# Host-packed projection and gate tiles, and the second pair's loads behind the first pair's hash, in a fused bucketed-attention and mixture-of-experts kernel

## The chip, the cores and the metric

The kernel runs on one core of one Trainium2 chip. The metric is the device time of one execution in microseconds (us), the median of several runs; lower is better. Engines are named as in the profile: PE is TensorE's matmul side and PEld its weight loads, DVE is VectorE, ACT is ScalarE, POOL is GpSimd, SP is SyncE, which only issues transfers. SPq, ACTq and POOLq are the instruction sequencers of those engines, each of which works in program order.

## The reference

Attention with a bucket mask feeds a top-1 mixture of experts. Cut to what matters here:

```python
# q, k, v: (2, 8, 768, 64); proj: (64, 6)
q_bits = (einsum('bhsd,dk->bhsk', q, proj) > 0)          # six sign bits per query and key
q_bucket = sum(q_bits * 2 ** arange(6)); ...             # the same for k
scores = where(q_bucket == k_bucket, q @ k.T / 8, -1e9)
attn = softmax(scores) @ v
x = attn.transpose(0, 2, 1, 3).reshape(2, 768, 512)
logits = x @ w_gate                                      # 8 experts
local_gate = sigmoid(x @ w_local)                        # < 0.5: fresh expert, else that of the token before
out[b, s] = p[e] * (relu(x[b, s] @ w1[e]) @ w2[e])       # e: the chosen expert, p: softmax of logits
```

## The kernel before

The 16 heads of the two batches are worked as 8 pairs; a pair's two heads lie on partitions 0 to 63 and 64 to 127. For a pair p, `lx.p.0` and `lx.p.1` load the transposed queries and keys (`xq`, `xk`: 128 x 768 float32, 384 KB each) from HBM. `hash.p` multiplies both by the projections `hw` on PE (tile `hb`), takes the signs on DVE (`bt`, L184) and scales them on ACT into `br` (L187). `bd.p.j.a` copies the bits by four small transfers (39 KB each, L190) into rows 51 to 76 of the operands `b`, where the scores get the mask as a second matmul over 64 rows. `hi` and `lo` split queries and keys into a rounded part `hx` (L197 on DVE or POOL, L195 on ACT) and its remainder `lx` (L205). `s1` forms the scores of one query block for the row maximum (PE, L213; DVE reduces into `mx`, L222); `ma`, `mb`, `mc` turn the maximum into one more row of the operand `b`; `s2` forms the transposed scores, ACT takes their exponent into `pt`; `pv` multiplies by the values. `ug` multiplies a finished pair's output by `iw`, a tile that holds an identity of 128 columns and 18 columns of gate weights for each of four pairs (128 x 4 x 146), which yields the transposed output and the router's logits in one matmul. Routing, a scatter into slots by expert and the eight experts' two matmuls follow; that part fills the span from about 265 us.

Nothing is reordered at run time. One string, `ORDER`, lists every part in the order in which its instructions go into the engines' programs, and `MOVED` says where a part doesn't run on its first engine; `lx.1.0` and `lx.1.1` are issued from ACT's sequencer, `lx.0.0`, `lx.0.1`, `lhw` and `lcs` from SP's. `busy.2` stands for four matmuls on the zeroed tile `Fl` into a buffer nobody reads; ORDER has ten of them ahead of `hash.0` (40 matmuls) and eight between `hash.0` and `hash.1` (32). They go in order like any other PE instruction, so PE reaches a hash only after the fillers ahead of it. The first `busy` waits for the memset of `Fl` on DVE (L536), which stands behind the memset of `hw` (L535).

`hw` is a 128 x 32 tile: zeros, and the 64 x 6 projections twice for each head. Before, DVE clears it and `lhw` copies the projections in by two transfers, whose rows are runs of six floats. `iw` is cleared by POOL in `clear` (L560), its identities come by `iwc` (L572) and its gate columns by `iwl.1` and `iwl.0` (L568), long before the first `ug`.

`hash.0` takes its bits on DVE; behind it on DVE stand, in this order, `hi.0.0`, `ident`, `hi.1.1` (which reads `xk` of the second pair), `lo.0.1`, and the sign step of `hash.1`; then the reductions of `s1` begin. On PE, `hash.1` stands behind the 32 fillers and ahead of eight more and the first `s1`. On ACT, `hash.0` is followed by `bd.0.0.1` and `bd.0.0.0`, then by `hash.1`, whose `br` reuses the buffer that the four `bd.0` copies read.

Of the kernel before, what the change touches and what calls it, by code (L numbers as in the profile page):

```python
# [19 lines left out]


ORDER = """
lx.0.0 busy.2 lx.0.1 busy.2 busy.2 busy.2 lhw busy.2 busy.2 hi.0.1 busy.2 lcs busy.2 lx.1.0 lx.1.1 busy.2 busy.2
hash.0 hi.0.0 busy.2 ident busy.2 bd.0.1.1 busy.2 hi.1.1 lo.0.1 bd.0.0.1 lo.0.0 busy.2 bd.0.0.0 bd.0.1.0 busy.2
load_v.0.2 busy.2 busy.2 busy.2 hash.1 busy.2 busy.2 s1.0.0.0 busy.2 s1.0.0.1 s1.0.1.0 hi.1.0 lo.1.0 busy.2 lx.2.1
busy.2 s1.0.1.1 bd.1.0.0 busy.2 bd.1.0.1 s1.0.2.0 busy.2 s1.0.2.1 busy.2 busy.2 clear busy.2 busy.2 load_v.0.0
s1.0.3.0 ma.0.0 busy.2 s1.0.3.1 busy.2 busy.2 busy.2 bd.1.1.1 busy.2 mb.0.0 s1.0.4.0 busy.2 lx.2.0 load_v.0.3 s1.0.4.1
# [1 line left out]
s1.1.0.1 busy.2 s1.1.1.0 s2.0.2.0 s1.1.1.1 busy.2 load_v.0.5 load_v.0.1 s1.1.2.0 hi.2.1 s2.0.4.0 load_v.0.4 lx.3.0  # L29
mf.0.0 mc.0.1 s2.0.3.0 s1.1.2.1 busy.2 s2.0.1.1 bd.2.1.0 s1.1.3.0 s2.0.0.1 busy.2 s1.1.3.1 s2.0.4.1 s1.1.4.0 bd.2.1.1  # L30
busy.2 padd.0.1.0 s2.0.2.1 bd.2.0.1 s1.1.4.1 vsum.0 hi.2.0 s2.0.5.1 s1.1.5.0 s1.1.5.1 pv.0.0.0 bd.2.0.0 mf.0.1
pv.0.1.0 padd.0.1.1 pv.0.0.1 pv.0.1.1 s1.2.0.0 s2.0.5.0 s2.0.3.1 s1.2.0.1 s1.2.1.0 pv.0.2.0 padd.0.2.0 ma.1 lx.3.1 iwc
pv.0.2.1 hash.3 io flat.0.1 flat.0.0 mb.1 s1.2.1.1 padd.0.3.0 padd.0.2.1 s1.2.2.0 s1.2.2.1 hi.3.1 bd.3.0.0 bd.3.0.1
pv.0.3.0 pv.0.3.1 pv.0.4.1 hi.3.0 padd.0.3.1 lo.2.0 padd.0.4.1 mc.1 bd.3.1.1 padd.0.4.0 pv.0.4.0 pv.0.5.1 bd.3.1.0
s1.2.3.0 s2.1.1.0 padd.0.5.1 s2.1.0.0 s1.2.3.1 padd.1.1.0 s2.1.2.0 s2.1.2.1 s1.2.4.0 s2.1.1.1 padd.0.5.0 s2.1.0.1
# [1 line left out]
padd.1.2.1 pv.1.0.1 pv.1.0.0 pv.1.1.0 pv.1.2.0 s1.3.0.1 s2.1.5.1 padd.1.3.0 s2.1.4.1 s1.3.1.0 s2.1.4.0 lx.4.1 s2.1.3.1  # L37
load_v.1.3 ma.2 s1.3.1.1 sa.0 padd.1.3.1 hash.4 flat.1.1 flat.1.0 mb.2 sb.0 pv.1.1.1 pv.1.2.1 bd.4.1.0 lo.3.0 pv.1.3.0
pv.1.3.1 padd.1.4.1 s1.3.2.0 s1.3.2.1 lx.5.0 s1.3.3.0 pv.1.4.1 bd.4.0.0 bd.4.0.1 pv.1.4.0 mc.2 pv.1.5.1 pv.1.5.0
s1.3.3.1 hi.4.1 iwl.1 ot.1 s2.2.0.0 padd.1.4.0 s2.2.1.1 s1.3.4.0 lo.3.1 bd.4.1.1 padd.1.5.0 s2.2.2.1 iwl.0 s2.2.1.0  # L40
padd.1.5.1 s1.3.4.1 s1.3.5.0 lx.5.1 pv.2.0.0 s1.3.5.1 s2.2.3.0 hi.4.0 s2.2.3.1 s2.2.2.0 s2.2.0.1 s2.2.4.0 sa.1 ma.3
padd.2.1.0 hash.5 mb.3 padd.2.1.1 sb.1 padd.2.2.0 mc.3 pv.2.0.1 pv.2.1.1 pv.2.1.0 pv.2.2.0 mf.2 pv.2.2.1 s1.4.0.0
padd.2.2.1 s2.2.5.1 s2.3.0.0 s2.2.5.0 s2.2.4.1 bd.5.0.0 s2.3.0.1 padd.2.3.0 lo.4.0 lo.4.1 s1.4.0.1 load_v.1.1 lx.6.0
# [38 lines left out]
def moved(kind, *where):  # L82
    return MOVED.get(kind, {}).get(where, 0)
# [35 lines left out]
def tile_kernel(ctx, tc, qT, kT, v, proj, wg, w1, w2, cst, out):  # L119
    nc = tc.nc  # L120
# [21 lines left out]
    hw = const.tile([128, 32], F32, name="hw")  # L142
    iw = const.tile([128, 4, 146], F32, name="iw")
# [21 lines left out]
    def queue(kind, *where):  # L165
        return (nc.sync, nc.scalar, nc.gpsimd)[moved(kind, *where)]
# [365 lines left out]
    warm = const.tile([128, 1], F32, name="warm")  # L532
    nc.vector.memset(warm, 0.0)
    nc.scalar.activation(out=warm, in_=warm, func=ACTF.Exp)
    nc.vector.memset(hw, 0.0)  # L535
    nc.vector.memset(Fl.bitcast(F32), 0.0)  # L536
    for t in B[0]:
        nc.vector.memset(t.bitcast(F32), 0.0)
# [10 lines left out]
                                 rhs=Fl[64 * i:64 * i + 64, 0:384], tile_position=(64 * i, 0))  # L549

    def lhw():
        for h in range(2):
            queue("lhw").dma_start(out=hw[64 * h:64 * h + 64, 13 * h:13 * h + 12].rearrange("p (a c) -> p a c", a=2),
                                   in_=proj.unsqueeze(1).to_broadcast([64, 2, 6]))

    def lcs():
        queue("lcs").dma_start(out=cs, in_=cst[:, 0:200])

    def clear():
        nc.gpsimd.memset(iw, 0.0)  # L560
        nc.gpsimd.memset(ones, 1.0)
        nc.gpsimd.memset(zr.bitcast(F32), 0.0)

    def ident():
        nc.vector.tensor_copy(out=idr, in_=idf)

    def iwl(h):
        nc.sync.dma_start(out=iw[64 * h:64 * h + 64, :, 128 + 9 * h:137 + 9 * h],  # L568
                          in_=wg.rearrange("(a b d) e -> b d a e", b=2, d=64)[h])

    def iwc():
        nc.sync.dma_start(out=iw[:, :, 0:128], in_=cst[:, 8:136].unsqueeze(1).to_broadcast([128, 4, 128]))  # L572
    XA, HLE, OHE = [], [], []

    def onehot(tag, o):
# [19 lines left out]
    def ugh(p, half):  # L595
        ug(p, (half,))
    parts = {f.__name__: f for f in (
        bd, busy, clear, fill_slots, fill_some, flat, hash, hi, hle, ident, io, iwc, iwl, lcs, lhw, lo, load_v, lx,
        ma, mb, mc, mf, ohe, ot, oth, padd, pv, s1, s2, sa, sah, sb, sbh, split_h, split_l, step, ug, ugh, vsum, xa)}
    with tc.manual_schedule():  # L600
        for part in ORDER.split():
# [114 lines left out]
    with tc.If(n_ovf > 0):  # L716
# [7 lines left out]
        for b in range(2):  # L724
# [13 lines left out]
            for q in range(6):  # L738
                nc.gpsimd.indirect_dma_start(
                    out=xo[:, :], out_offset=bass.IndirectOffsetOnAxis(ap=so[:, q:q + 1], axis=0),  # L740
                    in_=XT[b][:, q], in_offset=None, bounds_check=5 * CAP - 1, oob_is_err=False)
# [33 lines left out]
```

## Time and profile before

| | us |
|---|---|
| median of 3 runs | 465.82 |
| the runs | 465.82, 466.21, 463.77 |
| device time of the profiled execution | 469.77 |
| its span, first to last instruction | 467.9 |
| PE busy in it | 437.9 (94%) |
| DVE busy in it | 303.4 (65%) |
| ACT busy, POOL busy in it | 203.4 (43%), 177.7 (38%) |

The profile is of one execution with the recorder on, and its device time is 3.95 us above the median of the others. All starts are counted from the span's first instruction. PE's busy share contains the fillers, so it doesn't say how much of PE's time does work.

### The profile page before, as it was taken

To read this page: it belongs to the slowest core of one execution; us is meant where nothing else is said; L and a number is where in the kernel's file an instruction comes from. 1 tells how busy PE (TensorE), PEld (TensorE's weight loads), DVE (VectorE), ACT (ScalarE), POOL (GpSimd) and SP (SyncE) were. 2 spreads that over 40 slices of the span, in tenths; PEclk is the share of its full clock that TensorE was granted. 3 is DMA by queue.
4 is the path that set the end of the run, shared out by engine and by line. 5 is a ranking of instruction groups with operands and counts; after the bars stand their busy time and mean duration, and the time that the engine had idled before them with its cause. 6 is when DMAs were issued, how large, how long until landed. Compare 5 with 4: busy or idle time off the path is not lost.

```text
span 467.9 us, 8276 instructions
## 1 busy us (share of the span) xinstructions
PE 437.9 (94%) x3316; PEld 343.4 (73%) x3316; DVE 303.4 (65%) x440; ACT 203.4 (43%) x277; POOL 177.7 (38%) x127
## 2 busy tenths in 40 slices
PE   8999999999999997999987389999999999999993
PEld 7886466776667484666554389898989988999982
DVE  4988895647676867887668948473737464647210
ACT  1144354643636171453245037473636363736310
POOL 3468456397579474255357530101010102010101
PEclk9999999999999998999999569999999999999998
DMA  3532111121050020402047529966676757666000
GB/s 144 163 107 72 50 59 47 37 62 48 6 170 2 35 73 2 181 1 87 36 156 242 179 69 317 322 194 222 207 237 206 230 191 255 222 217 223 36 2 31
DMA packets 41577, 60.17 MB, mean 129 GB/s; under 512 B 5949, under 2 KB 24093, under 8 KB 41536
## 3 DMA queue, kind: packets, MB, share of 16 engines
q1 hardware_dynamic: 38010, 50.54, 33.6%
q0 software_dynamic: 2272, 6.31, 3.6%
q10 hardware_dynamic: 1254, 2.76, 1.9%
q8 instruction: 27, 0.44, 0.4%
q14 instruction: 14, 0.11, 0.1%
HBM read 47.66 MB, written 11.56 MB: 127 GB/s over the span
## 4 chain that ended last, share of the span: by engine, by line
PE 44%; issue 36%; DVE 10%; POOL 4%; DMA 1%; ACT 1%; POOLq 0%; ACTq 0%; SPq 0%; DVEq 0%
PE s L213 21%; PE pv L275 13%; POOL out L698 4%; PE busy L548 3%; DVE rw L436 2%; PE ug L369 2%; DVE mx L222 2%; DVE sp L268 1%; PE st L327 1%; PE xt L612 1%; PE hb L181 1%; DMA PI<-xs 1%; DVE nf L229 1%; PE pv L282 1%; DVE lx L205 1%
## 5 line engine op out<-in xcount | busy, mean ns | idle before, releaser
L222 DVE TENSOR_REDUCE mx<-s 128x2 f32<-128x768 f32 x96 | 88.7, 953 | 37.1 <-PE s L213 36.4
L646 DVE TENSOR_TENSOR wl<-st,wh 128x1024 fp32r<-128x1024 f32 x60 | 71.8, 1221 | 61.5 <-ACT wh L645 61.4
L268 POOL TENSOR_TENSOR sp<-sp,pt 128x768 f32<-128x768 f32 x42 | 79.5, 1905 | 61.0 <-DVE sp L268 30.3
L261 ACT ACTIVATE pt<-s 128x768 f32<-128x768 f32 x96 | 73.2, 811 | 65.1 <-PE s L213 60.0
L645 ACT ACTIVATE wh<-st 128x1024 fp32r<-128x1024 f32 x64 | 66.5, 1059 | 46.9 <-DMA st<-w 27.0
L213 PE MATMUL s<-hx 64*128 64x384 f32 x384 | 71.3, 366 | 1.2 <-DVE mx L222 1.1
L676 PE MATMUL hps<-xH,wh 128*128 128x256 f32 x256 | 70.8, 278 | 0.7 <-ACT xH L709 0.7
L676 PE MATMUL hps<-xH,wl 128*128 128x256 f32 x256 | 70.6, 277 | 0.0
L676 PE MATMUL hps<-xL,wh 128*128 128x256 f32 x256 | 70.4, 277 | 0.0
L275 PE MATMUL pv<-pt,v 128*64 128x384 f32 x384 | 70.2, 504 | 0.0
L698 POOL DMA_INDIRECT out<-y,xsl x14 | 15.7, 1124 | 143.4 <-ACT y L697 143.4
L213 PE MATMUL s<-b,b 64*128 64x384 f32 x384 | 65.4, 334 | 0.1
L213 PEld LDWEIGHTS s<-hx 64*128 64x128 f32 x384 | 36.4, 184 | 23.8 <-issue 9.9
L694 PE MATMUL yps<-wh,hL 128*128 128x512 f32 x128 | 50.4, 394 | 0.3 <-DVE hL L681 0.3
L694 PE MATMUL yps<-wh,hH 128*128 128x512 f32 x128 | 50.7, 396 | 0.0
L275 PEld LDWEIGHTS pv<-pt,v 128*64 128x64 f32 x384 | 25.4, 139 | 34.0 <-issue 33.2
L694 PE MATMUL yps<-wl,hH 128*128 128x512 f32 x128 | 49.9, 390 | 0.0
L676 PEld LDWEIGHTS hps<-xH,wh 128*128 128x128 f32 x256 | 48.1, 188 | 1.2 <-ACT xH L709 1.0
L676 PEld LDWEIGHTS hps<-xH,wl 128*128 128x128 f32 x256 | 48.1, 188 | 0.3
L676 PEld LDWEIGHTS hps<-xL,wh 128*128 128x128 f32 x256 | 48.0, 188 | 0.0
L213 PEld LDWEIGHTS s<-b,b 64*128 64x128 f32 x384 | 36.6, 185 | 0.4 <-DMA b<-br 0.4
L213 PE MATMUL s<-hx,lx 64*128 64x384 f32 x192 | 32.6, 333 | 0.0
(161 smaller groups left out, 628.1 us busy)
## 6 DMA issues: line engine op xcount, KB each, us to landing
st<-w SPq DMA_DIRECT2D x64, 512.0 KB
xs<-z SPq DMA_DIRECT2D x8, 513.0 KB
xsl<-xs SPq DMA_DIRECT2D x7, 514.0 KB
v<-v SPq DMA_DIRECT2D x12, 256.0 KB
xq<-qT SPq DMA_DIRECT2D x5, 384.0 KB
xk<-kT SPq DMA_DIRECT2D x5, 384.0 KB
xq<-qT ACTq DMA_DIRECT2D x3, 384.0 KB
xk<-kT ACTq DMA_DIRECT2D x3, 384.0 KB
```

Of the source, the lines that this page charges most:

```text
L213: nc.tensor.matmul(out=sc[:, h, 0:384], lhsT=w[r, cols[0]], rhs=x[r, cols[1]], tile_position=(64 * h, 0), start=first and n == 0, stop=las ...
L222: nc.vector.tensor_reduce(out=MX[p][:, kh, i // 3, :, i % 3], in_=sc[:, :, 0:384], axis=AX.X, op=ALU.max)
L261: nc.scalar.activation(out=pt.rearrange("p (a q) -> p a q", a=2), in_=sc[:, :, 0:384], func=ACTF.Exp, scale=0.125)
L268: eng.tensor_tensor(out=SP[p, h], in0=PT[p, 0, h] if kt == 1 else SP[p, h], in1=PT[p, kt, h], op=ALU.add)
L275: nc.tensor.matmul(out=PV[p][64 * h:64 * h + 64, half, 0:384], lhsT=V[b, kt][:, pp * 128 + 64 * h:pp * 128 + 64 * h + 64], rhs=PT[p, kt, h ...
L369: nc.tensor.matmul(out=t[:, half, j * 146:j * 146 + 146], lhsT=OT[p][:, q * 128:q * 128 + 128], rhs=iw[:, pp])
L548: nc.tensor.matmul(out=IDLE[0][:, i, 0:384], lhsT=Fl[64 * i:64 * i + 64, 0:128], rhs=Fl[64 * i:64 * i + 64, 0:384], tile_position=(64 * i, 0))
L645: nc.scalar.activation(out=H, in_=st, func=ACTF.Copy)
L646: (eng or nc.vector).tensor_tensor(out=L, in0=st, in1=H.bitcast(F32), op=ALU.subtract)
L676: nc.tensor.matmul(out=hps[:, k], lhsT=w[:, c, fs], rhs=x[:, c], start=(n == 0), stop=(n == 11))
L694: nc.tensor.matmul(out=yps, lhsT=h[:, k, ts], rhs=w[:, k], start=(n == 0), stop=(n == 23))
L698: i = nc.gpsimd.indirect_dma_start(out=out, out_offset=bass.IndirectOffsetOnAxis(ap=pi[:, t, 1:2].bitcast(I32), axis=0), in_=y, in_offset= ...
```

## The change

Both small operands are laid out by the host. `proj` arrives as the finished 128 x 32 tile and `wg` as the finished 128 x 584 tile, identities included, so that `lhw` and `iwl` are one transfer each; `iwc`, the memset of `hw` and the memset of `iw` are gone. In ORDER, `lhw` moves from behind `lx.0.1` to the very front, and `lx.1.0` and `lx.1.1` move from ahead of `hash.0` to directly behind it. The numbers of fillers ahead of `hash.0` and between the two hashes stay 40 and 32.

```diff
 ORDER = """
-lx.0.0 busy.2 lx.0.1 busy.2 busy.2 busy.2 lhw busy.2 busy.2 hi.0.1 busy.2 lcs busy.2 lx.1.0 lx.1.1 busy.2 busy.2
-hash.0 hi.0.0 busy.2 ident busy.2 bd.0.1.1 busy.2 hi.1.1 lo.0.1 bd.0.0.1 lo.0.0 busy.2 bd.0.0.0 bd.0.1.0 busy.2
+lhw lx.0.0 busy.2 lx.0.1 busy.2 busy.2 busy.2 busy.2 busy.2 hi.0.1 busy.2 lcs busy.2 busy.2 busy.2
+hash.0 lx.1.0 lx.1.1 hi.0.0 busy.2 ident busy.2 bd.0.1.1 busy.2 hi.1.1 lo.0.1 bd.0.0.1 lo.0.0 busy.2 bd.0.0.0 bd.0.1.0 busy.2
...
-pv.0.1.0 padd.0.1.1 ... pv.0.2.0 padd.0.2.0 ma.1 lx.3.1 iwc
+pv.0.1.0 padd.0.1.1 ... pv.0.2.0 padd.0.2.0 ma.1 lx.3.1
...
-s1.3.3.1 hi.4.1 iwl.1 ot.1 s2.2.0.0 padd.1.4.0 s2.2.1.1 s1.3.4.0 lo.3.1 bd.4.1.1 padd.1.5.0 s2.2.2.1 iwl.0 s2.2.1.0
+s1.3.3.1 hi.4.1 iwl ot.1 s2.2.0.0 padd.1.4.0 s2.2.1.1 s1.3.4.0 lo.3.1 bd.4.1.1 padd.1.5.0 s2.2.2.1 s2.2.1.0
...
-    nc.vector.memset(hw, 0.0)
...
     def lhw():
-        for h in range(2):
-            queue("lhw").dma_start(out=hw[64 * h:64 * h + 64, 13 * h:13 * h + 12].rearrange("p (a c) -> p a c", a=2),
-                                   in_=proj.unsqueeze(1).to_broadcast([64, 2, 6]))
+        queue("lhw").dma_start(out=hw, in_=proj)
...
     def clear():
-        nc.gpsimd.memset(iw, 0.0)
...
-    def iwl(h):
-        nc.sync.dma_start(out=iw[64 * h:64 * h + 64, :, 128 + 9 * h:137 + 9 * h],
-                          in_=wg.rearrange("(a b d) e -> b d a e", b=2, d=64)[h])
-
-    def iwc():
-        nc.sync.dma_start(out=iw[:, :, 0:128], in_=cst[:, 8:136].unsqueeze(1).to_broadcast([128, 4, 128]))
+    def iwl():
+        nc.sync.dma_start(out=iw.rearrange("p a c -> p (a c)"), in_=wg)
...
+    hw, iw = np.zeros((128, 32), np.float32), np.zeros((128, 4, 146), np.float32)
+    g = np.concatenate([inputs["moe_w_gate"], inputs["moe_w_local"]], axis=1).reshape(4, 2, D, 9)
+    iw[:, :, 0:128] = np.eye(128)[:, None]
+    for h in range(2):
+        r = slice(64 * h, 64 * h + 64)
+        hw[r, 13 * h:13 * h + 12] = np.tile(inputs["proj"], (1, 2))
+        iw[r, :, 128 + 9 * h:137 + 9 * h] = g[:, h].transpose(1, 0, 2)
```

## Rows read from the trace of the kernel before

**Rows 1.** The page: the span in 40 slices, PE and the granted clock.
```profile
PE   8999999999999997999987389999999999999993
...
PEclk9999999999999998999999569999999999999998
```

**Rows 2.** Chain of waits from 8 to 36 us: start us, us, what.
```profile
8.23 0.83 PE hb L181 x8
...
9.08 0.63 DVE bt L184
...
10.38 1.40 ACTq L190
...
11.82 2.07 DMA b<-br
```

**Rows 3.** Timeline of PE from 1.5 us: start, length (us), engine, line, operation, tiles, count.
```profile
1.78 6.45 PE L548 MATMUL busy<-Fl 64*128 64x384 f32 x40 [1.78 <-DVE Fl L536]
...
11.92 0.52 PE L181 MATMUL hb<-xq,hw 128*32 128x384 f32 x2
...
13.52 0.34 PE L213 MATMUL s<-hx 64*128 64x384 f32 x2
13.93 0.44 PE L213 MATMUL s<-b,b 64*128 64x384 f32 x2
```

**Rows 4.** Fillers' weight loads, two stretches: ns min/median/max, first and last start.
```profile
L548 PEld LDWEIGHTS busy<-Fl x8: 327/330/332, 6.4 to 7.4; 64*128 64x128 f32 x8
...
L548 PEld LDWEIGHTS busy<-Fl x38: 182/184/186, 8.9 to 13.0; 64*128 64x128 f32 x38
```

**Rows 5.** Line of the hash on PE, 0 to 14 us: its semaphore wait.
```profile
L181 PEldq EVENT_SEMAPHORE  x1: 51/51/51, 7.2 to 7.2; - x1
```

**Rows 6.** Timeline of DVE from 0 us.
```profile
0.83 0.09 DVE L535 MEMSET hw<- 128x32 f32 x1
1.02 0.70 DVE L536 MEMSET Fl<- 128x768 f32 x1
...
6.54 0.56 DVE L197 CAST hx<-xk 128x768 fp32r<-128x768 f32 x1 [3.20 <-DMA xk<-kT]
...
10.68 2.58 DVE L205 TENSOR_TENSOR lx<-xk,hx 128x768 fp32r<-128x768 f32 x1
...
14.41 6.20 DVE L222 TENSOR_REDUCE mx<-s 128x2 f32<-128x768 f32 x7 [0.62 <-PE s L213]
```

**Rows 7.** Timeline of ACT and its sequencer from 0 us.
```profile
0.72 0.42 ACTq L171 DMA_DIRECT2D xq<-qT  x1
...
1.24 0.38 ACTq L171 DMA_DIRECT2D xk<-kT  x1
...
9.73 0.62 ACT L187 ACTIVATE br<-bt,cs 128x384 fp32r<-128x384 f32 x1 [7.06 <-DVE bt L184]
...
14.04 0.62 ACT L187 ACTIVATE br<-bt,cs 128x384 fp32r<-128x384 f32 x1 [3.69 <-DMA b<-br]
14.09 0.34 ACTq L171 DMA_DIRECT2D xk<-kT  x1
```

**Rows 8.** Windows: stretch, engines' busy us, granted clock, DMA share, GB/s.
```profile
2.50:6.00 3.50, 3.50 (x24) 3.50 (x24) 0.73 (x2) 0.17 (x1) 0.98 (x2) 1.00 1.01 395
...
6.75:11.50 4.75, 4.75 (x50) 3.88 (x50) 2.77 (x6) 0.62 (x1) 1.25 (x1) 1.00 0.00 0
...
24.50:25.50 1.00, 1.00 (x15) 1.00 (x14) 1.00 (x2) 0.00 (x0) 0.00 (x0) 1.00 1.08 397
```

**Rows 9.** Timeline of DVE at 54.7 us: the same step with POOL idle.
```profile
54.71 0.95 DVE L205 TENSOR_TENSOR lx<-xq,hx 128x768 fp32r<-128x768 f32 x1
```

**Rows 10.** Instructions on the tile iw: ns min/median/max, first and last start.
```profile
L369 PE MATMUL ug<-iw,ot x96: 285/288/393, 102.8 to 251.1; 128*128 128x146 f32 x96
L568 SPq DMA_DIRECT2D iw<-wg x2: 667/674/682, 79.3 to 81.0; - x2
L560 POOL MEMSET iw<- x1: 587/587/587, 17.2 to 17.2; 128x584 f32 x1
L572 SPq DMA_DIRECT2D iw<-cst x1: 422/422/422, 38.6 to 38.6; - x1
```

**Rows 11.** PE's longest idle stretches (in brackets), and the clock around one.
```profile
177.25 0.22 PE L236 MATMUL tp<-idr,nf 128*24 128x128 f32 x1 [1.79 <-DVE nf L230]
...
264.62 0.80 PE L453 MATMUL tk<-cs,rZ 128*8 128x128 f32 x3 [9.31 <-DVE rZ L443]
...
176.00:178.00 2.00, 0.75 (x9) 0.25 (x9) 1.97 (x5) 0.00 (x0) 1.92 (x2) 1.00 0.00 0
...
256.50:257.00 0.50, 0.00 (x0) 0.90 0.00 0
257.00:257.50 0.50, 0.00 (x0) 0.50 0.00 0
```

More of the change, by code (lines that the diff above doesn't have):

```diff
@@ L31 @@
 busy.2 padd.0.1.0 s2.0.2.1 bd.2.0.1 s1.1.4.1 vsum.0 hi.2.0 s2.0.5.1 s1.1.5.0 s1.1.5.1 pv.0.0.0 bd.2.0.0 mf.0.1
-pv.0.1.0 padd.0.1.1 pv.0.0.1 pv.0.1.1 s1.2.0.0 s2.0.5.0 s2.0.3.1 s1.2.0.1 s1.2.1.0 pv.0.2.0 padd.0.2.0 ma.1 lx.3.1 iwc
+pv.0.1.0 padd.0.1.1 pv.0.0.1 pv.0.1.1 s1.2.0.0 s2.0.5.0 s2.0.3.1 s1.2.0.1 s1.2.1.0 pv.0.2.0 padd.0.2.0 ma.1 lx.3.1
 pv.0.2.1 hash.3 io flat.0.1 flat.0.0 mb.1 s1.2.1.1 padd.0.3.0 padd.0.2.1 s1.2.2.0 s1.2.2.1 hi.3.1 bd.3.0.0 bd.3.0.1
@@ L597, in tile_kernel @@
     parts = {f.__name__: f for f in (
-        bd, busy, clear, fill_slots, fill_some, flat, hash, hi, hle, ident, io, iwc, iwl, lcs, lhw, lo, load_v, lx,
+        bd, busy, clear, fill_slots, fill_some, flat, hash, hi, hle, ident, io, iwl, lcs, lhw, lo, load_v, lx,
         ma, mb, mc, mf, ohe, ot, oth, padd, pv, s1, s2, sa, sah, sb, sbh, split_h, split_l, step, ug, ugh, vsum, xa)}
@@ L761 @@
         "v": np.ascontiguousarray(inputs["v"].transpose(0, 2, 1, 3)).reshape(B, S, H * D),
-        "proj": np.ascontiguousarray(inputs["proj"]),
-        "wg": np.concatenate([inputs["moe_w_gate"], inputs["moe_w_local"]], axis=1),
+        "proj": hw,
+        "wg": iw.reshape(128, 584),
         "w1": np.ascontiguousarray(inputs["moe_w1"]),
```

## The prediction

> **What bounds the kernel now.** I read the page's slices first. PE is busy nine tenths or more of nearly every slice from the first to the experts, and the clock is granted in full except around 256 to 277 us [rows 1]. Nothing in that row says which part of PE's time is work, because fillers count as busy, so the change has to be read where it acts: the first 16 us. There the chain of waits runs through the first pair's hash on PE at 8.23, its sign step on DVE at 9.08, the issue of the bits from ACT at 10.38, their flight from 11.82, and the score matmul that takes them at 13.93 [rows 2, 3]. From then on PE works without a long gap, so what arrives late at 13.93 is late at the end.
>
> The point to see is what set 8.23. PE ran 40 fillers from 1.78 without a break and came to the hash when they were done [rows 3]. The transfers that the hash needs were in by 7.25: that is when its wait was passed in PE's sequencer [rows 5]. The queries and keys were earlier still, since DVE, which sat waiting for the keys, started on them at 6.54 [rows 6]. So the first pair's loads had 0.9 us to spare, and the fillers, not the loads, decide when the first hash goes.
>
> **The change, part by part.**
>
> The memset of `hw` goes. It stood ahead of the memset of `Fl`, for which the first filler waits: 0.09 us long, and 0.19 us from its start to that of `Fl` [rows 6]. Between 0.09 and 0.19 is gained; I take 0.1. The hash of the first pair then starts at 8.13.
>
> The first pair's loads no longer share the transfer engines with the second pair's, and `hw` comes in one piece ahead of them. Worth nothing by itself: both land sooner, at a hash that still stands behind 40 fillers. The cover is those 0.9 us; without it (fillers that end sooner) see the third rival. The issue of `lhw` ahead of `lx.0.0` delays the latter by one issue, about 0.4 us as the issues beside it [rows 7], which the same cover takes.
>
> The second pair's loads move from 0.72 us to behind the first hash's ACT step. Nothing stops them until ACT's sequencer has passed that step: a load that stands behind the same step of the second hash was issued 0.05 us after the step began, 14.09 against 14.04 [rows 7]. The step began at 9.73 and will begin at 9.63, so the two loads are issued from 9.68 to 10.5 (0.42 and 0.38 us each) [rows 7].
>
> When are they in? Before, four such loads, 1.573 MB, went out from 0.72 and the keys were in DVE's hands at 6.54, which is 5.82 us [rows 6, 7]. At the 395 GB/s of the stretch from 2.5 to 6 us [rows 8] the bytes take 3.98 us of that; 1.84 us is lead, ramp and landing. Half the bytes take 1.99 us, so 3.83 in all, and the second pair is in at 9.68 + 3.83 = 13.5. The transfer engines are idle from 6.75 to 11.5 [rows 8], so nothing is in the way but the first pair's bits (four times 39 KB). Lower end: 0.9 us from issue to the first bytes (0.72 to about 1.6) and the rate at once, which is 12.6. Upper end: a single queue that gets half the rate, 198 GB/s, which is 9.68 + 1.84 + 3.97 = 15.5. SP's queue alone moved 397 GB/s from 24.5 to 25.5 [rows 8], so I stay near the middle, at 13.5.
>
> What waits for them: on PE, `hash.1`, which started at 11.92 [rows 3] and would be reached at 11.82. PE stands still for 13.5 - 11.82 = 1.7 us, and with it the eight fillers and the first score matmul behind it. From the hash to that matmul it took 1.60 us (11.92 to 13.52) and 0.17 more to the one with the bits (half of a 0.34 us matmul, two being in flight at once); before, that one stood till 13.93 for the bits [rows 3]. After, it comes at 13.5 + 1.60 + 0.17 = 15.27, and is 15.27 - 13.93 = 1.34 us later. The wait for the bits that was there, 0.24 us, is swallowed in that.
>
> Are the bits in by 15.27? ACT's sequencer now has the two loads ahead of them, which end at 10.5 instead of the 10.38 at which the bits started. With the first issue of 1.40 and a flight of 2.07 from the start of the second [rows 2], they are in at 14.0, or, if they queue behind the loads' last bytes at 13.5, at 15.6. The first costs nothing; the second adds 0.3. I take nothing, and 0.3 for the range.
>
> On DVE the step `hi.1.1` waits for the same keys. Queued behind it are the remainder `lo.0.1`, the sign step of `hash.1` and all reductions. From 13.5: 0.56 for the rounding [rows 6], 0.95 for the remainder (2.58 before, when POOL worked beside it; 0.95 with POOL idle, which it will be) [rows 6, 9], about 0.6 for the sign step: 15.6. The first reduction, which followed its matmul's start by 0.48 (13.93 to 14.41 [rows 3, 6]), would start at 15.75. DVE is thus just in time, and PE's 1.34 stands.
>
> `iw`: its clearing on POOL (0.59), one issue of 0.42 and two of 0.67 fall away, and one load of 299 KB takes their place near 79 us [rows 10]. At 397 GB/s that is 0.75 us of transfer, and the first use is at 102.8 [rows 10]. Nothing waits for `iw` on either side; no gain, no loss. If the cover of over 20 us were gone, it would cost a flight, 1.84 + 0.75 = 2.6.
>
> The sum: 467.9 us of span + 1.3 = 469.2, and by the same difference 469.77 + 1.3 = 471.1 for the profiled execution. The runs' median is 3.95 below the profiled one; 465.82 + 1.3 = **467.1 us**. Bounds of this case: loads at 12.6 give 12.6 + 1.77 - 13.93 = +0.4, so 466.2; bits at 15.6 give +1.7, 467.5; half rate gives 15.5 + 1.77 - 13.93 = +3.3, 469.2.
>
> The rule "issue the DMA early, do compute, wait on its semaphore late" in the Trainium skill (DMA: Bandwidth & Descriptors, Rules for kernel authors) speaks against moving these loads. With that page's fit for another kind of queue, 2.0 us plus bytes at 436 GB/s, the flight would be an estimated 3.8 us, and the sum would be the same 1.3.
>
> **The rivals.**
>
> The clock falls in the new gap (slower). PE has kept its clock in an idle stretch of 1.79 us and lost it about 1.6 us into one of 9.31, at 256.9 [rows 11]. A gap of 1.7 us lies between the two. At the start the fillers still took 330 ns a pair at 7.4 us and 184 from 8.9 [rows 4], though the granted clock reads full over both; by their pace that is the lower and the upper of the two levels, and the climb took 5.6 us or more from 1.78. If it has to climb again, some 5.8 us of PE run at half pace and lose 2.9: +4.2, 470.0. For it: fillers and scores fill PE there. Against it: PE works without a break up to the gap and the kept 1.79 us is longer. It decides as soon as the gap grows past what was kept.
>
> The Trainium skill (TensorE: Matmul & The Clock Gate, Why this matters for your kernels) warns of idle gaps between bursts of matmuls for this reason; rows 11 show both outcomes.
>
> Half rate on one queue (slower): 469.2 as above. Against it, the 397 GB/s of SP alone.
>
> The fillers end early (faster). Without the recorder PE may reach its upper level sooner. If all 20 pairs took 184 ns, they would end at 1.68 + 3.7 = 5.4; before, the hash would then wait for `hw` until 7.25. After, the first pair is in by about 1.15 + 3.83 = 5.0 and the hash goes at 5.4. The score matmul follows the hash by 5.70 before and by 15.27 - 8.13 = 7.14 after: 12.95 against 12.54, -0.4, 465.4. It decides where the fillers end before 5.8. Against it: the profile shows them slow to 7.4.
>
> The rule to coalesce small transfers in the Trainium skill (the DMA page, same section) would make `hw` the gain; here 7.25 against 8.23 says that nothing waited for it.
>
> The delay is hidden (no change): the second pair is in by 11.9, or the 1.3 us are taken up by a later wait. The first needs 2.2 us for what I put at 2.9 at the least; for the second I find no place. 465.7.
>
> **How the numbers follow.** Forecast 0.62, clock 0.13, half rate 0.06, early fillers 0.12, hidden 0.07. A measurement of this kernel tells about 0.5%, 2.3 us, from no change: 463.5 and 468.1 are the bounds. Slower by more: the clock, half rate, and 0.05 of the forecast with the runs' own spread of 2.4 us: 0.24. Faster by more: half of early fillers with that spread, 0.06. The rest, 0.70. The range takes in half rate and early fillers with half that spread below, and leaves out the clock: 464.2 to 469.4. The forecast's own is 466.0 to 468.1.
>
> **What would show it.** Hash of the first pair on PE at about 8.1, still straight behind a filler; the second pair's loads issued by ACT near 9.7; an idle stretch of PE of 1.3 to 1.8 us before `hash.1`, ended by a load; `hi.1.1` ended by the same; first reduction near 15.7. I am wrong if the gap is under 0.5 us, if fillers after it take 330 ns a pair, or if a later stage gives the 1.3 us back.

## The result, and the profile after

The changed kernel takes 468.14 us (median of 22 runs, 465.56 to 472.26) against 465.88 for the kernel before (22 runs, 463.37 to 469.43). The ratio is 1.0052, 95% interval 1.0030 to 1.0074: slower by 1.4 to 3.4 us. The forecast was 467.1. Some executions are in a slower state; ratios, here and below, leave those out and are not quotients of the two medians, so the two differ a little.

The chain of waits of the changed kernel, from 8 to 17 us, against [rows 2]; columns are start us, us, what:

```profile
8.00 0.83 PE hb L181 x8
...
8.85 0.63 DVE bt L184
...
9.50 0.40 ACT br L187
...
9.94 4.22 DMA xk<-kT
...
14.21 0.84 PE hb L181 x4
...
15.94 0.35 PE s L213 x4
```

The chain no longer goes through the bits. It leaves the first hash by way of its ACT step, behind which the second pair's keys are issued at 9.94, waits 4.22 us for them, and comes back on PE at the second half of the second hash. The same on PE's timeline, against [rows 3]:

```profile
1.74 6.26 PE L547 MATMUL busy<-Fl 64*128 64x384 f32 x40 [1.74 <-DVE Fl L535]
7.93 0.52 PE L181 MATMUL hb<-xq,hw 128*32 128x384 f32 x2
...
8.71 3.05 PE L547 MATMUL busy<-Fl 64*128 64x384 f32 x32
12.75 0.84 PE L181 MATMUL hb<-xq,hw 128*32 128x384 f32 x4 [0.99 <-DMA xq<-qT]
14.21 0.84 PE L181 MATMUL hb<-xk,hw 128*32 128x384 f32 x4 [0.62 <-DMA xk<-kT]
14.98 0.96 PE L547 MATMUL busy<-Fl 64*128 64x384 f32 x8
15.78 0.34 PE L213 MATMUL s<-hx 64*128 64x384 f32 x2
15.95 0.34 PE L213 MATMUL s<-b,b 64*128 64x384 f32 x2
```

The first hash still comes straight behind the 40 fillers. The second one is broken in two: PE waits 0.99 us for the queries, works 0.84, waits 0.62 for the keys. The score matmul with the bits is at 15.95, against 13.93 before [rows 3]: 2.02 us later, although the first hash was 0.23 us earlier. ACT's sequencer, SP's and DVE, against [rows 6, 7]:

```profile
9.50 0.62 ACT L187 ACTIVATE br<-bt,cs 128x384 fp32r<-128x384 f32 x1 [7.28 <-DVE bt L184]
9.51 0.40 ACTq L171 DMA_DIRECT2D xq<-qT  x1
9.94 0.44 ACTq L171 DMA_DIRECT2D xk<-kT  x1
10.48 2.28 ACTq L190 DMA_DIRECT2D b<-br  x2
...
1.18 0.42 SPq L171 DMA_DIRECT2D xq<-qT  x1
...
12.01 1.09 SPq L175 DMA_DIRECT2D v<-v  x2
...
6.03 0.56 DVE L197 CAST hx<-xk 128x768 fp32r<-128x768 f32 x1 [2.73 <-DMA xk<-kT]
...
14.19 0.56 DVE L197 CAST hx<-xk 128x768 fp32r<-128x768 f32 x1 [4.12 <-DMA xk<-kT]
14.67 0.95 DVE L205 TENSOR_TENSOR lx<-xk,hx 128x768 fp32r<-128x768 f32 x1
...
16.34 6.19 DVE L222 TENSOR_REDUCE mx<-s 128x2 f32<-128x768 f32 x7 [0.19 <-PE s L213]
```

DVE stands still for 4.12 us at `hi.1.1` and is then just in time: its first reduction follows PE's matmul with 0.19 us of idle. The delay travels on. The first matmul on `iw` is at 105.1 us against 102.8 [rows 10]:

```profile
L369 PE MATMUL ug<-iw,ot x96: 286/288/392, 105.1 to 253.4; 128*128 128x146 f32 x96
```

The last matmul on `iw` is 2.3 us later too, 253.4 against 251.1. The ends of the two profiled executions don't show it: the span is 467.3, shorter than the 467.9 of before. In this one execution the clock fell less; from 235 to 285 us it was granted 0.80 before (first row) and 0.86 here (second row; the number ahead of the last two):

```profile
235.00:285.00 50.00, 36.96 (x248) 29.45 (x248) 37.05 (x84) 19.21 (x28) 23.46 (x18) 0.80 0.52 174
235.00:285.00 50.00, 38.10 (x268) 29.58 (x269) 40.12 (x87) 19.85 (x30) 23.84 (x19) 0.86 0.56 183
```

Over the whole span the granted clock was 0.983 here and 0.971 before. Among the 22 runs of the changed kernel a mean granted clock that is lower by 0.01 goes with 2.9 us more (a straight line through them, correlation -0.80), so the 0.012 between the two executions are worth an estimated 3.5 us, more than the loss. One execution of each kernel is thus no measure of a difference of 2 us. The runs are, and the early stage of the trace, up to the first matmul on `iw`, says where it comes from.

### The profile page after: what moved, and what is told of

Same layout as the page of the kernel before. It is cut to its first block, busy times and chain, and to the rows that moved or that the text cites. A ratio compares the mean times of both kernels' runs of the same rounds, so it can differ in the third digit from the quotient of the medians.

```text
span 467.3 us, 8266 instructions
## 1 busy us (share of the span) xinstructions
PE 436.6 (93%) x3316; PEld 341.2 (73%) x3316; DVE 303.6 (65%) x439; ACT 203.5 (44%) x277; POOL 176.2 (38%) x126
## 4 chain that ended last, share of the span: by engine, by line
PE 45%; issue 36%; DVE 10%; POOL 4%; DMA 2%; ACT 1%; POOLq 0%; SPq 0%; DVEq 0%; ACTq 0%
PE s L213 20%; PE pv L275 13%; POOL out L691 4%; PE busy L547 3%; PE ug L369 2%; DVE sp L268 2%; DVE rw L436 2%; DVE mx L222 2%; DMA PI<-xs 1%; PE st L327 1%; PE hb L181 1%; DMA xk<-kT 1%; PE xt L605 1%; PE pv L282 1%; DVE nf L229 1%
## 5 line engine op out<-in xcount | busy, mean ns | idle before, releaser
L275 PE MATMUL pv<-pt,v 128*64 128x384 f32 x384 | 69.2, 497 | 0.0
```

What stands on the lines that cost most here:

```text
L275: nc.tensor.matmul(out=PV[p][64 * h:64 * h + 64, half, 0:384], lhsT=V[b, kt][:, pp * 128 + 64 * h:pp * 128 + 64 * h + 64], rhs=PT[p, kt, h ...
```

## The experiments

Theory: the whole loss is PE's wait for the second pair at the second hash, and it reaches the end undiminished. Rivals: the new layouts or the one load of `iw` cost something; or the loss comes from the transfers and not from the wait. A later question was why the second pair's flight (from the issue of its queries to the use of its keys) is longer than the 3.83 us of the forecast. Each experiment's runs are compared with runs of the kernel before taken beside them. The last column of the table at the end gives the difference at equal clock: a straight line in the granted clock, with one slope (2.3 to 2.9 us per 0.01), is put through the runs of both kernels, and the distance between them is read off, with its 95% interval. (For the comparison above the clocks of the other kernel's runs are not on record.)

**The move undone.** The changed kernel with the two loads ahead of the first hash again.

```diff
-... hi.0.1 busy.2 lcs busy.2 busy.2 busy.2
-hash.0 lx.1.0 lx.1.1 hi.0.0 ...
+... hi.0.1 busy.2 lcs busy.2 lx.1.0 lx.1.1 busy.2 busy.2
+hash.0 hi.0.0 ...
```

> The changed kernel with the second pair's two loads put back ahead of the first hash; host layouts, the single iw load and the projections in front stay. Theory (the whole loss is PE's wait for the second pair): the second hash is reached with its operands long in, no idle stretch of PE there, 465.7 us, 0.1 to 0.3 below the kernel before. Rival (the loss comes from the new layouts, the 299 KB iw load or the projections ahead of the queries): it stays near 468.

Measured: 466.72 against 466.59, ratio 1.0007 (0.9971 to 1.0043). PE's timeline there:

```profile
8.00 0.52 PE L181 MATMUL hb<-xq,hw 128*32 128x384 f32 x2
...
11.79 0.52 PE L181 MATMUL hb<-xq,hw 128*32 128x384 f32 x2
...
12.57 0.98 PE L547 MATMUL busy<-Fl 64*128 64x384 f32 x8
...
13.77 0.45 PE L213 MATMUL s<-b,b 64*128 64x384 f32 x2
```

The second hash waits for nothing and the score matmul is 5.77 us behind the first hash, as before (8.16 to 13.93 in PE's timeline). Layouts, the single load of `iw` and the projections in front are worth nothing that shows, on either side: at equal clock the difference is 0.1 us (-0.6 to 0.9).

**The move alone.** The kernel before with nothing but the new place of `lx.1.0` and `lx.1.1`.

> The kernel before with nothing changed but the place of the second pair's two loads, now behind the first hash. Theory (wait): 2.0 to 2.4 us slower than before, second hash ending near 15.2 us. Rival (layouts): no slower than before.

Measured: 467.89 against 466.59, ratio 1.0027 (0.9995 to 1.0059). By that ratio the times don't settle it. At equal clock they do, 1.8 us slower (1.1 to 2.5), and the trace shows the wait in full:

```profile
1.78 5.41 PE L548 MATMUL busy<-Fl 64*128 64x384 f32 x40 [1.78 <-DVE Fl L536]
...
12.04 0.84 PE L181 MATMUL hb<-xq,hw 128*32 128x384 f32 x4 [1.06 <-DMA xq<-qT]
13.65 0.84 PE L181 MATMUL hb<-xk,hw 128*32 128x384 f32 x4 [0.77 <-DMA xk<-kT]
...
15.40 0.34 PE L213 MATMUL s<-b,b 64*128 64x384 f32 x2
```

In this execution the 40 fillers took 5.41 us and not 6.45 [rows 3]. The hash began at 7.12, and the score matmul came 8.28 us behind it. Their weight loads drop from 326 to 184 ns near 5.2 us here, and in the kernel before only after 7.4 [rows 4]. When PE comes to its upper pace thus differs from one execution to the next, by about 1 us of the first hash's start, so from here on I compare distances from the first hash, and only then times.

**Fillers in the place of the wait.** The kernel before, 24 more fillers ahead of the second hash.

```diff
-load_v.0.2 busy.2 busy.2 busy.2 hash.1 ...
+load_v.0.2 busy.2 busy.2 busy.2 busy.12 hash.1 ...
```

> The kernel before with 24 more fillers ahead of the second hash, which hold PE there as long as the changed kernel's wait does (12 pairs of 186 ns, 2.2 us), with all loads where they were. Theory (what PE loses ahead of the second hash reaches the end undiminished): the first score matmul with the bits 2.0 us later, 2.0 us slower. Rival (a later stage gives it back, and the changed kernel's loss comes from its transfers): no change, within 0.5 us.

Measured: 468.91 against 465.68, ratio 1.0060 (1.0033 to 1.0087). From 7.76 to 15.41 the distance is 7.65, 1.9 more than before. With every load in its old place, as much time lost ahead of the second hash gives at least as large a loss at the end (1.5 to 4.1 us). The rival that a later stage gives it back is out. At equal clock the loss is 3.0 us (2.5 to 3.5), some 1 us more than the 1.9 of the trace; where the rest comes from isn't shown.

**What makes the flight long: two experiments on the value loads.** In the changed kernel two value loads of 256 KB go out on SP at 12.0 and share the transfer engines with the end of the second pair's keys. They were moved ahead of everything (behind `lcs`), and then behind `bd.1.1.1`.

```diff
# early
-... lcs busy.2 busy.2 busy.2
+... lcs load_v.0.2 load_v.0.0 busy.2 busy.2 busy.2
# late
-... bd.1.1.1 busy.2 mb.0.0 ...
+... bd.1.1.1 load_v.0.2 load_v.0.0 busy.2 mb.0.0 ...
```

> The changed kernel with the two value loads of 256 KB that go out at 12 us moved to SP's queue behind the constants, so that they are in before the second pair's loads are issued. Theory (the second pair's 4.66 us of flight are 0.8 longer than reckoned because those value loads share the transfer engines): the keys land at 13.2 to 13.5 instead of 14.17, and the kernel is 1.1 to 1.4 slower than before, about 1 us faster than the changed one. Rival (one queue alone is this slow): keys still at 14.0 to 14.2, 2.3 slower than before.

> The same two value loads moved the other way, behind the second pair's bits on SP's queue, near 17 us. Theory (they share the engines with the second pair): keys at 13.2 to 13.5, 1.1 to 1.4 slower than before. Rival (one queue alone is this slow): keys at 14.0 to 14.2, 2.3 slower. Should the two value loads then be late for their sum on POOL at 31 us, it shows as a wait there.

Measured: early 469.37 against 466.59, ratio 1.0060 (1.0031 to 1.0090); late 468.06, ratio 1.0049 (1.0015 to 1.0084). In DVE's timelines the keys are taken at 14.22 and at 13.63:

```profile
14.22 0.56 DVE L197 CAST hx<-xk 128x768 fp32r<-128x768 f32 x1 [4.33 <-DMA xk<-kT]
```

```profile
13.63 0.56 DVE L197 CAST hx<-xk 128x768 fp32r<-128x768 f32 x1 [3.78 <-DMA xk<-kT]
```

From the issue of the queries (9.33 and 9.29) that is 4.89 and 4.34 us, against 4.68 in the changed kernel. My theory of contention with the values, by which the keys would come at 13.2 to 13.5 in both, fell as far as it was to explain the long flight: with the values out of the way early, the flight was no shorter. A smaller share of theirs can't be told from one execution each (see the spread of flights in the next section), nor from the times, 2.1 us (1.3 to 2.8) and 1.6 us (0.9 to 2.4) slower at equal clock. The sum on POOL didn't wait for the late values.

**Only the keys late.** The changed kernel with `lx.1.0` ahead of the first hash and `lx.1.1` behind it.

```diff
-... lcs busy.2 busy.2 busy.2
-hash.0 lx.1.0 lx.1.1 hi.0.0 ...
+... lcs busy.2 lx.1.0 busy.2 busy.2
+hash.0 lx.1.1 hi.0.0 ...
```

> The changed kernel with the second pair's queries loaded ahead of the first hash again and only its keys behind it. Theory (the first load of a queue needs 3.0 to 3.3 us from its issue, each further one 1.2 to 2.1 more, and PE waits for the last): keys in at 12.6 to 12.9, the score matmul with the bits at 14.4, 0.4 to 0.8 us slower than before and about 1.5 faster than the changed kernel. Rival (the flight is set by something else than the load ahead in the queue, such as the bits or the memory): keys at 13.5 or later, at least 1.3 slower.

Measured: 465.88 against 466.31, ratio 0.9991 (0.9966 to 1.0017). The chain of waits:

```profile
7.31 0.83 PE hb L181 x8
...
8.82 3.10 DMA xk<-kT
...
11.96 0.84 PE hb L181 x4
```

One load behind the hash flies 3.10 us, as expected. PE has come to the second hash at 11.02 and does the queries' half alone; the keys' half follows when they land. The distance to the score matmul (7.24 to 13.71) is 6.47, 0.7 more than before. That loss doesn't show in the times, also not at equal clock (0.0, -0.6 to 0.6); 0.4 to 0.8 was expected. The second load of the queue is what brings most of the wait: PE takes it up 1.5 us after the first in the changed kernel (12.75 and 14.21), 1.2 to 2.2 in the others.

**Fewer fillers.** In the kernel before, 28 ahead of the first hash instead of 40; in the changed kernel, 20.

```diff
# the kernel before
-... hi.0.1 busy.2 lcs busy.2 lx.1.0 lx.1.1 busy.2 busy.2
+... hi.0.1 lcs lx.1.0 lx.1.1 busy.2
# the changed kernel
-lhw lx.0.0 busy.2 lx.0.1 busy.2 busy.2 busy.2 busy.2 busy.2 hi.0.1 busy.2 lcs busy.2 busy.2 busy.2
+lhw lx.0.0 busy.2 lx.0.1 busy.2 busy.2 busy.2 busy.2 hi.0.1 lcs
```

> The kernel before with 28 fillers instead of 40 ahead of the first hash and nothing else changed. Theory (fillers decide, with 0.9 us in hand): the hash goes at 7.2, when its operands are in, 0.7 to 1.0 us faster. Rival (the loads decide already): no change.

> The changed kernel with 20 fillers instead of 40 ahead of the first hash. Theory: the first pair, alone on its queue, is in at 5.3 to 6.0, the hash goes then, 2.0 to 2.6 us sooner than in the changed kernel; the second pair still comes 4.3 to 4.9 us after its issue, so the wait at the second hash stays and the kernel ends level with the one before, within 0.5 us, some 2 us faster than the changed one. Rival (the lower clock at the start eats the gain): as slow as the changed kernel.

Measured: 465.62 against 465.68, ratio 0.9995 (0.9965 to 1.0025), and 467.21, ratio 1.0017 (0.9987 to 1.0047). Both expectations were too good. At equal clock the first is 0.1 us faster (-0.4 to 0.6), the second 0.9 us slower (0.3 to 1.5). In the first the hash waits for the projections and starts only 0.62 us earlier, at 7.54:

```profile
7.54 0.52 PE L181 MATMUL hb<-xq,hw 128*32 128x384 f32 x2 [1.10 <-DMA hw<-proj]
```

In the second the first hash goes at 5.24, but only with the queries: its keys are taken by DVE at 6.00 and by PE at 6.02. PE is also still at its lower pace (1.49 us for a half, 0.84 at the second hash). DVE's sign step, at 8.85 in the changed kernel, comes at 7.56, so of 2.7 us 1.3 are left, and the second pair's flight is 5.24 us (8.22 to 13.46):

```profile
5.24 1.49 PE L181 MATMUL hb<-xq,hw 128*32 128x384 f32 x4
...
6.00 0.56 DVE L197 CAST hx<-xk 128x768 fp32r<-128x768 f32 x1 [2.70 <-DMA xk<-kT]
6.02 1.48 PE L181 MATMUL hb<-xk,hw 128*32 128x384 f32 x4
...
13.48 0.84 PE L181 MATMUL hb<-xk,hw 128*32 128x384 f32 x4 [1.31 <-DMA xk<-kT]
...
15.24 0.34 PE L213 MATMUL s<-b,b 64*128 64x384 f32 x2
```

So a first hash that is 2.7 us earlier brought the score matmul forward by 0.7.

**Both queues, and no load behind the hash.** The first pair's queries on SP and keys on ACT, the second pair's right behind them, 20 fillers.

```diff
-lhw lx.0.0 busy.2 lx.0.1 busy.2 busy.2 busy.2 busy.2 busy.2 hi.0.1 busy.2 lcs busy.2 busy.2 busy.2
-hash.0 lx.1.0 lx.1.1 hi.0.0 ...
+lhw lx.0.0 lx.0.1 lcs lx.1.0 lx.1.1 busy.10 hi.0.1
+hash.0 hi.0.0 ...
-    "lx": {(1, 0): 1, (1, 1): 1, ...
+    "lx": {(0, 1): 1, (1, 0): 0, (1, 1): 1, ...
```

> The changed kernel with the first pair's queries on SP's queue and its keys on ACT's, the second pair's loads right behind them on the same two queues and not behind the hash, and 20 fillers instead of 40 ahead of the first hash. Theory (the fillers, not the loads, decide when the first hash goes; two queues carry a pair faster than one): first pair in by 4.5 us, first hash at 5.1, second pair in before the second hash, first score matmul with the bits near 12.0 instead of 13.9, 1.5 to 2 us faster than before. Rival (PE at its lower clock for longer, or the loads after all): no faster than before.

Measured: 464.31 against 465.68, ratio 0.9972 (0.9944 to 1.0001): by that not clearly faster; at equal clock 1.0 us faster (0.4 to 1.5), less than expected. The first pair was in later than expected too, the queries at 5.6 and not by 4.5, and the hash started at 5.75 and not 5.1. The score matmul is at 11.87, and what it waits for now is the bits, as in the kernel before. The chain:

```profile
1.18 4.44 DMA xq<-qT
...
8.32 1.40 ACTq L190
...
9.77 2.06 DMA b<-br
...
11.87 0.45 PE s L213 x2
```

**The bits that are read first, first.** On top of that, `bd.0.1.0` and `bd.0.0.0` ahead of `bd.0.1.1` and `bd.0.0.1`, 18 fillers ahead of the first hash and 24 between the hashes, `lhw` behind the first pair's loads.

```diff
-lhw lx.0.0 lx.0.1 lcs lx.1.0 lx.1.1 busy.10 hi.0.1
-hash.0 hi.0.0 busy.2 ident busy.2 bd.0.1.1 busy.2 hi.1.1 lo.0.1 bd.0.0.1 lo.0.0 busy.2 bd.0.0.0 bd.0.1.0 busy.2
-load_v.0.2 busy.2 busy.2 busy.2 hash.1 ...
+lx.0.0 lx.0.1 lhw lcs lx.1.0 lx.1.1 busy.9 hi.0.1
+hash.0 hi.0.0 busy.2 ident busy.2 bd.0.1.0 busy.2 hi.1.1 lo.0.1 bd.0.0.0 lo.0.0 bd.0.0.1 bd.0.1.1 busy.2
+load_v.0.2 busy.2 busy.2 hash.1 ...
```

> The kernel of both queues, in which the score matmul waited for the bits and no longer for a load, with the two bit copies that this matmul reads issued first on each queue, 18 fillers ahead of the first hash, 24 between the hashes, and the projections behind the first queries. Theory (after the loads the bits' issue is next): the matmul with the bits comes 0.7 to 1.2 us earlier, near 11.0, and the kernel is 2.2 to 3.2 us faster than the one before. Rival (the bits' flight or the lower clock at the start decides): no faster than the kernel of both queues, 464.3.

Measured: 463.81 against 466.31, ratio 0.9959 (0.9931 to 0.9988): faster than the kernel before, by 0.6 to 3.2 us. The intervals don't tell it from the kernel of both queues. The score matmul no longer waits:

```profile
1.18 4.03 DMA hw<-proj
...
5.34 0.85 PE hb L181 x8
...
10.18 0.47 PE s L213 x4
```

It comes at 10.21, earlier than the 11.0 expected and 1.66 before that of both queues. Of this 0.41 is the earlier first hash, 1.04 the shorter way from there to the second (3.09 against 4.13, with eight fillers fewer), and 0.21 the wait for the bits that is gone. What the order of the bits is worth by itself no run shows, since the fillers were changed with it.

The distances of all kernels, from PE's timelines (start of the first hash, of the score matmul with the bits, and of the first matmul on `iw`, which is the first `ug`), beside the ratios and the differences at equal clock:

| kernel | first hash | score matmul | distance | first `ug` | ratio to before | us at equal clock |
|---|---|---|---|---|---|---|
| before | 8.16 | 13.93 | 5.77 | 102.8 | 1 | 0 |
| changed | 7.93 | 15.95 | 8.02 | 105.1 | 1.0052 | - |
| move undone | 8.00 | 13.77 | 5.77 | 102.7 | 1.0007 | 0.1 (-0.6 to 0.9) |
| move alone | 7.12 | 15.40 | 8.28 | 104.3 | 1.0027 | 1.8 (1.1 to 2.5) |
| values early | 7.75 | 15.99 | 8.24 | 105.1 | 1.0060 | 2.1 (1.3 to 2.8) |
| values late | 7.71 | 15.40 | 7.69 | 104.2 | 1.0049 | 1.6 (0.9 to 2.4) |
| 24 fillers more | 7.76 | 15.41 | 7.65 | 104.3 | 1.0060 | 3.0 (2.5 to 3.5) |
| keys late | 7.24 | 13.71 | 6.47 | 102.5 | 0.9991 | 0.0 (-0.6 to 0.6) |
| before, 28 fillers | 7.54 | 13.30 | 5.76 | 102.2 | 0.9995 | -0.1 (-0.6 to 0.4) |
| changed, 20 fillers | 5.24 | 15.24 | 10.00 | 104.4 | 1.0017 | 0.9 (0.3 to 1.5) |
| both queues | 5.75 | 11.87 | 6.12 | 101.1 | 0.9972 | -1.0 (-1.5 to -0.4) |
| bits first | 5.34 | 10.21 | 4.87 | 99.6 | 0.9959 | -2.1 (-2.7 to -1.4) |

In all twelve traces the first `ug` follows the score matmul by 88.8 to 89.4 us, whatever was done ahead of it. What the score matmul loses or gains is thus still there some 89 us later. At the end less of it can show: bits first has its score matmul 3.7 us earlier and is 2.1 us faster. Whether the executions without the profiler start otherwise or a later stage gives time back isn't shown.

## Why the prediction was right, point by point

The direction and the mechanism were right. The memset's 0.1 us: the first filler started at 1.74 instead of 1.78, so 0.04; the rest of the hash's 0.23 us comes from fillers that took 6.26 and not 6.45. The first pair's loads gained nothing, since the hash stood behind its fillers as before. The loads were issued at 9.51, where 9.68 was reckoned. PE, DVE and the bits did what the steps said: the keys were followed by the score matmul 1.74 us later (14.21 to 15.95), where 1.60 + 0.17 was reckoned; the remainder took 0.95; the bits were in on time. `iw` cost and brought nothing that shows in the move undone. On the profile of before, two readings were loose: the slices show a clock below nine tenths near 180 us as well [rows 1], which touches nothing here; and the one wait of rows 5 doesn't say that all operands are in (with 20 fillers it was passed at 4.1 us, and the keys came at 6.0).

The stall cost more than PE's idle time. PE stood still for 0.99 + 0.62 = 1.61 us, but the distance grew by 2.25. The eight matmuls of a whole hash run the queries' and the keys' half side by side and take 0.78 us (11.79 to 12.57 in the move undone). Broken in two, the keys' half alone takes as long (14.21 to 14.98), so the queries' half, done ahead of it, saved nothing: 1.61 us idle and 0.84 for that half, less the 0.24 that the score matmul had waited for the bits, are 2.21. The sum took the whole hash as still to do when the keys land and came out right in that, by luck: it didn't foresee the break.

The step that was mis-sized is "Half the bytes take 1.99 us, so 3.83 in all". It measured 4.70 from 9.51 to PE's start on the keys at 14.21. With the issue 0.17 us earlier than reckoned, the keys were 0.7 us late against 13.5, and the score matmul stood at 15.95 instead of 15.27: +2.02 against +1.34. The distance from the hash grew by 2.25 (8.02 against 5.77). The 2.26 us of the medians agree with it, but closer than their interval of 1.4 to 3.4 warrants. The rate was wrong. I took 395 GB/s, which four loads on two queues had moved [rows 8]. A pair alone on one queue was slower in two ways: at the start 307 GB/s with hardly anything beside it (first row below), and behind the hash a slow first microsecond, 397 GB/s for 1.5 us, and a slow end, with bits and values beside it (the others; last number GB/s).

```profile
2.50:5.00 2.50, 2.50 (x18) 2.50 (x18) 0.70 (x1) 0.00 (x0) 0.98 (x2) 1.00 0.93 307
10.50:11.50 1.00, 1.00 (x16) 0.94 (x12) 0.00 (x0) 0.00 (x0) 1.00 (x1) 1.00 0.77 184
11.50:13.00 1.50, 0.51 (x6) 0.14 (x4) 0.00 (x0) 0.00 (x0) 0.35 (x1) 1.00 1.02 397
13.00:14.25 1.25, 0.63 (x6) 0.04 (x4) 0.06 (x1) 0.00 (x0) 0.00 (x0) 1.00 0.92 268
```

The end is slow without the values too. With the values early, the rate had fallen to 62 GB/s from 13.5 to 14.0, ahead of the keys' use at 14.22:

```profile
13.50:14.00 0.50, 0.00 (x0) 1.00 0.23 62
```

The sum also left out what shares the transfer engines. It put the bits at nothing, though their four times 39 KB are an estimated 0.4 us at 395 GB/s, and it looked at the engines only up to 11.5 us [rows 8], while the value loads go out at 12.0. No run takes the bits away, so their share isn't shown.

Over the five kernels with both loads behind the hash the flight was 4.34 to 5.24 us (to DVE's start on the keys). Much of that spread needs no edit: in three kernels (changed, values late, 20 fillers) the first pair's loads go out at 1.18 with the same transfers around them, and DVE took the keys at 6.03, 5.34 and 6.00, flights of 4.85, 4.16 and 4.82 us. The row of values late:

```profile
5.34 0.56 DVE L197 CAST hx<-xk 128x768 fp32r<-128x768 f32 x1 [2.04 <-DMA xk<-kT]
```

What makes one execution's flight 0.7 us longer than another's stays open.

The rivals: the clock didn't fall in the gap. The fillers and the score matmuls behind it ran at their old pace (eight in 0.96, 0.98 before; 0.34 a matmul), and the gap came in two pieces of 0.99 and 0.62 us with work between them. One queue at half rate didn't come true as such, but the truth lay between it and the forecast. The early fillers exist as a spread of the start (hash at 7.12 to 8.16 with 40 fillers), and with 28 fillers the projections did hold up the hash at 7.54; without the trim, nothing waited for them. The delay was not hidden: fillers in the place of the wait cost at least as much, and the first `ug` came as much later as the score matmul did (2.3 and 2.0 us).

The rule of the Trainium skill to issue a transfer early and wait late (DMA: Bandwidth & Descriptors, Rules for kernel authors) held here: the same loads cost nothing that shows ahead of the hash (ratio 1.0007) and 0.5% behind it.

## What to carry to other kernels

A load is worth moving back only if the work that it then makes room for waits for something, and nothing waits at a fixed number of fillers; first look what released the instruction that is to gain. Reckon a moved load's flight from a flight of the same make (so many loads on one queue, from first issue to first use), not from a rate seen with more in flight. A stall that breaks a step in two can cost more than the idle time shows; compare the distance between two fixed points of the program instead. Where a hand-written order puts all engines in one chain, microseconds lost at the start are still missing far behind it, and the next term of that chain (here the bits, which the score matmul waited for once the loads were early) is where to look after the loads.

## What the runs showed of the hardware

A pair of 384 KB loads alone on one queue took 4.0 to 4.9 us from its first issue to DVE's start on the keys at the head of the kernel (constants of 100 KB and the projections beside it) and four such loads on two queues 5.8 to 6.2: half the bytes don't take half the time. The Trainium skill (DMA: Bandwidth & Descriptors, Issuing engines are not separate DMA queues) says that spreading transfers over queues saves only issue time; here the 307 GB/s of one queue stand against the 395 of two [rows 8], though SP alone also reached 397 at 24.5 us [rows 8], with three value loads and one of queries behind each other. From 3 to 6 us SP alone moved 374 with the value loads queued behind the first pair (values early), and four loads on both queues 402 (both queues). So how much is queued may count more than how many queues; no run changes one of the two alone.

The 16 KB of projections queued behind one 384 KB load, with three more such loads on the two queues, took 4.03 us to be usable (last chain above). And PE's rise to its upper pace came at different times in different executions: 40 fillers took 5.41 to 6.45 us, while the granted clock in the profile reads 1.00 over both paces.
